# Retention and two feed-forward layers on one core: the layers in blocks of 384 tokens instead of 512 and 256

## The chip, the cores and the metric

The kernel runs on one core of a Trainium2 chip. The metric is the device time of one execution in microseconds (us). Engines are TensorE (PE in the rows; PEld is its weight load), VectorE (DVE), ScalarE (ACT), GpSimd (POOL) and SyncE (SP, which here only issues DMAs).

## The reference

A retention layer is followed by two feed-forward layers on 2304 tokens of 512 features.

```python
scores = scale * np.matmul(q, k.transpose(0, 1, 3, 2))      # 4 batches, 8 heads, 576 tokens, 64 wide
Dmat = np.where(rel >= 0, gamma[:, None, None] ** rel[None, :, :], 0.0)
x = np.matmul(scores * Dmat[None], v)                        # -> 2304 x 512
h = x @ w_in;  x = np.maximum(0.01 * h, h) @ w_out           # layer 1, d_ff 2048
h = x @ w_in2; out = (h - np.tanh(h)) @ w_out2               # layer 2, d_ff 2048
```

## The kernel before

**Arithmetic.** Each matmul operand is kept as a high and a low part (xh and xl; `w[:, 0]` and `w[:, 1]`; `g[:, 0]` and `g[:, 1]`), and each product is made of three matmuls: high by high, high by low, low by high.

**Tiling of the layers.** d_ff is 16 slices of 128, in 4 groups of 4 slices (`NG`, `GF`). A group `(m, g)` of layer `m` goes through all 2304 tokens in blocks; a step is one block and one slice `f`, so a block has 4 steps. Before the change a group has the token blocks 512, 512, 256, 512, 512 (five, 20 steps); the last group of all has the 256 at its end. The first group begins with six blocks of 256 (`EARLY`, `QW`), done two slices at a time during the retention (`unit_h`, `unit_o`), and goes on with one block of 256 and one of 512.

**A step.** `h_mm` (L194) makes h, 128 slice features by n tokens: 4 input chunks by 3 products, 12 matmuls n columns wide. `act_a` and `chain` make g from it. In layer 1 that is two ScalarE operations (L207, L208) and GpSimd's low part (L240). In layer 2, `act_a` has ScalarE's square, tanh and two more (L216 to L222) and GpSimd's product v (L218); `chain` has VectorE's subtraction (L233), product (L234) and predicated copy (L237), ScalarE's high part (L239) and GpSimd's low part (L240). `o_mm` (L266) adds the slice's share of the output in PSUM: in layer 1, 4 output chunks by 3 products, n columns wide; in layer 2, n/128 token chunks by 3 products, always 512 columns wide. After the fourth slice `evac` adds the sums into `acc` in SBUF (VectorE, L292; in a first group, copies at L288 and L290), in layer 1 n wide, in layer 2 always 512 wide. In layer 1's last group it also splits the result into xh (L296) and xl (L302); in layer 2's last it sends `acc` out.

**Order.** It is written out by hand (`manual_schedule`); each engine works through its queue in program order. In iteration s come `h_mm(s)`, `chain(s-1)`, `act_a(s)`, `o_mm(s-2)` (`LAG` is 2), up to four weight operations, `evac(s-2)`, the other weight operations, and the splits of weights. In the last four steps `act_a(s)` stands ahead of `chain(s-1)`, and the last four `o_mm` follow the last `h_mm`.

**Weights.** They come as 64-bit words and are narrowed by VectorE (L127 to L148) during layer 1, those of layer 2 partly to a scratch in DRAM and back (L163, L168). These operations are spread over the steps of a group. At its end each of the next group's 8 pieces is split: ScalarE's high part (L174), GpSimd's low part (L175), one piece in each of two steps, two in each of the next two, one in each of two more.

**Buffers.** PSUM has 3 tiles for h and 5 for the output sums, each 128 x 512; a g tile lives for three steps.

Of the kernel before, what the change touches and what calls it, by code (L numbers as in the profile page):

```python
# [33 lines left out]
def retention_moe_moe(  # L34
# [18 lines left out]
    NT, DM = out.shape  # L53
# [7 lines left out]
    NG = NF // GF  # L61
# [11 lines left out]

    QW, EARLY = 256, 6
    steps = []
    per_group = {}
    for m in range(2):
        for g in range(NG):  # L80
            big = [(t, 512) for t in range(0, NT - NT % 512, 512)]
            rest = [(NT - NT % 512, NT % 512)] if NT % 512 else []
            if (m, g) == (0, 0):
                blocks = [(t * QW, QW) for t in range(EARLY)]
                blocks += rest + [b for b in big if b[0] >= EARLY * QW]
            elif (m, g) == (1, NG - 1):
                blocks = big + rest
            else:
                blocks = big[:2] + rest + big[2:]
            first = len(steps)  # L90
            steps += [(m, g, t, n, f) for t, n in blocks for f in range(GF)]
            per_group[m, g] = (first, len(steps))
# [12 lines left out]
    def load_piece(key):  # L105
        m, kind, f = key
        src = ((w1i, w1o), (w2i, w2o))[m][kind][f]
        st = stage.tile([P, 512], I64 if wide else F32, tag="st", name="st")
        nc.sync.dma_start(out=st, in_=src)
        raw[key] = st  # L110
# [55 lines left out]
    def fetch_piece(key):  # L166
        w = cw_pool[0].tile([P, 512], F32, tag="cw", name="cw")
        nc.sync.dma_start(out=w, in_=kept.pop(key))  # L168
        half[key] = w

    def split_piece(key):
        wf = half.pop(key)
        wp = wring.tile([P, 2, 512], F32R, tag=f"w{key[1]}", name="wp")
        nc.scalar.activation(out=wp[:, 0, :], in_=wf, func=AF.Copy)  # L174
        nc.gpsimd.tensor_tensor(  # L175
            out=wp[:, 1, :], in0=wf, in1=wp[:, 0, :].bitcast(F32), op=ALU.subtract
        )
        wt[key] = wp

    def pieces_of(m, g):  # L180
        return [(m, kind, g * GF + f) for f in range(GF) for kind in range(2)]


    pools = {}
    hp, ga, tmp, ac_ps = {}, {}, {}, {}

    def h_mm(s):
        m, g, t0, n, f = steps[s]
        w = wt[m, 0, g * GF + f]
        ps = pools["h"](s)  # L190
        for kk in range(KK):
            cs = slice(kk * P, (kk + 1) * P)
            for i, (wi, x) in enumerate(((0, xh), (0, xl), (1, xh))):
                nc.tensor.matmul(  # L194
                    out=ps[:, :n], lhsT=w[:, wi, cs], rhs=x[:, kk, t0:t0 + n],
                    start=kk == 0 and i == 0, stop=kk == KK - 1 and i == 2,
                )
        hp[s] = ps

    def act_a(s):  # L200
        m, g, t0, n, f = steps[s]
        W, tp = pools["w"], pools["t"]
        h = hp[s][:, :n]
        if m == 0:
            a = tp.tile([P, W], F32, tag="u", name="a")
            gt = pools["g"].tile([P, 2, W], F32R, tag="g", name="g")
            nc.scalar.activation(out=a[:, :n], in_=h, func=AF.Prelu, alpha=0.01)  # L207
            nc.scalar.activation(out=gt[:, 0, :n], in_=h, func=AF.Prelu, alpha=0.01)  # L208
            tmp[s] = a, gt
            return  # L210
        u = tp.tile([P, W], F32, tag="u", name="u")
        v = tp.tile([P, W], F32, tag="v", name="v")
        t_ = tp.tile([P, W], F32, tag="t", name="t")
        q = tp.tile([P, W], F32, tag="q", name="q")
        mk = tp.tile([P, W], F32, tag="mk", name="mk")
        nc.scalar.activation(out=u[:, :n], in_=h, func=AF.Square)  # L216
        nc.scalar.activation(out=t_[:, :n], in_=h, func=AF.Tanh)  # L217
        nc.gpsimd.tensor_tensor(out=v[:, :n], in0=t_[:, :n], in1=u[:, :n], op=ALU.mult)  # L218
        nc.scalar.activation(  # L219
            out=q[:, :n], in_=u[:, :n], func=AF.Square, scale=math.sqrt(RHO_C), bias=qb[:, 0:1]  # L220
        )
        nc.scalar.activation(out=mk[:, :n], in_=u[:, :n], func=AF.Relu, bias=qb[:, 1:2])  # L222
        tmp[s] = (v, t_, q, mk)
# [83 lines left out]
    def split_order(keys):  # L307

        return sorted(keys, key=lambda k: (k[2] + LAG * k[1], k[1]))

    def piece_ops(keys, split=True, spare=()):


        ops, late = [], []
        for j, key in enumerate(keys):
            part = narrow_ops(key)
            if j + 2 < len(keys):
                part.append(lambda k=keys[j + 2]: load_piece(k))
            ops += part[:3] + late + part[3:]
            late = [lambda k=key: split_piece(k)] if split else []  # L320
            if key in spare:
                late = [lambda k=key: keep_piece(k)]
        return ops + late
# [303 lines left out]
    def layers():  # L627
        with ExitStack() as mc:
            pools["t"] = mc.enter_context(tc.tile_pool(name="t1", bufs=2))
            pools["g"] = mc.enter_context(tc.tile_pool(name="g1", bufs=3))  # L630
            cw_pool[0] = mc.enter_context(tc.tile_pool(name="c1", bufs=2 * GF + 3))
            ps_h = mc.enter_context(tc.tile_pool(name="ps_h1", bufs=3, space=PSUM))
            pools["h"] = lambda s: ps_h.tile([P, 512], F32, tag="h", name="h")
            pools["a"] = mc.enter_context(tc.tile_pool(name="ps_a1", bufs=5, space=PSUM))
            pools["w"] = 512
            early[0] = False

            plan, splits = {}, {}  # L640
            groups = list(per_group)
            free = n_early
            for q, nxt in zip(groups, groups[1:]):
                lo, hi = per_group[q]
                lo, last = max(lo, free), hi - GF
                keys = split_order(pieces_of(*nxt))

                kept_ones = [k for g in range(1, NG) for k in pieces_of(1, g)]
                a, b = (len(kept_ones) * (q[1] - i) // (NG - 2) for i in (1, 0))
                spare = kept_ones[max(a, 0):b] if q[0] == 0 and 0 < q[1] < NG - 1 else []  # L650
                if q[0]:
                    ops = [lambda k=k: fetch_piece(k) for k in keys]
                else:
                    ops = piece_ops(keys + spare, split=False, spare=spare)
                    plan.setdefault(lo, []).extend([lambda k=k: load_piece(k) for k in keys[:2]])
                free = max(hi if spare else last + 1, lo + 9)
                span = range(lo + 1, free)
                for j, op in enumerate(ops):
                    plan.setdefault(span[j * len(span) // len(ops)], []).append(op)
                for key in keys:  # L660
                    at = last + key[2] % GF + (1 if key[1] == 0 else 1 + LAG)
                    splits.setdefault(at, []).append(key)
            end = len(steps)
            for s in range(n_early, end):
                h_mm(s)
                tight = s >= end - GF
                if tight:
                    act_a(s)
                if s > n_early:
                    chain(s - 1)  # L670
                if not tight:
                    act_a(s)
                if n_early <= s - LAG < end - GF:
                    o_mm(s - LAG)
                ops = plan.get(s, [])
                for op in ops[:4]:
                    op()
                if n_early <= s - LAG < end - GF:
                    evac(s - LAG)
                for op in ops[4:]:  # L680
                    op()
                for key in splits.get(s, ()):
                    split_piece(key)

            for s in range(end - GF, end):
                o_mm(s)
                if s == end - GF:
                    chain(end - 1)
                evac(s)

    with tc.manual_schedule():
        retention()
        layers()
# [69 lines left out]
```

## Time and profile before

| what | us |
|---|---|
| median of 3 runs | 892.57 (891.94 to 893.65) |
| profiled execution | 891.21 |
| its span, first to last instruction | 889.4 |
| TensorE busy | 863.9 (97%) |
| VectorE, ScalarE, GpSimd busy | 532.8, 374.3, 422.5 |

Times in the timeline count from the start of the span. A matmul's own duration in the rows (389 ns at 512 columns) is its latency; matmuls overlap, so what one costs is read from start to start. The layers begin at about 162 us, layer 2 at about 488 us. "Idle before" in a row names the engine's waiting time and, behind the arrow, what ended it.

### The profile page before, as it was taken

Reading aid. Unit: us, or ns where it says so; the run is one execution under the profiler, and the core shown is the slowest. Engines: PE = TensorE matmul, PEld = TensorE weight load, DVE = VectorE, ACT = ScalarE, POOL = GpSimd, SP = SyncE. Lnnn points to the kernel's source line nnn. Section 1 sums busy time; section 2 is a strip of 40 time slices with the busy share of each in tenths; the row PEclk is TensorE's granted clock in tenths of the full one; section 3 lists DMA queues with packets and bytes.
Section 4 is the critical chain, followed back from the end, with each engine's and each line's share of the span. In section 5 each row is a group of like instructions: output and inputs, shape, how many; then the busy total and the mean of one; then the engine's idle time right before and its main releaser. Section 6 shows DMA issues by size and latency. Waiting matters only on the chain.

```text
span 889.4 us, 13456 instructions
## 1 busy us (share of the span) xinstructions
PE 863.9 (97%) x5152; PEld 740.8 (83%) x5152; DVE 532.8 (60%) x880; ACT 374.3 (42%) x751; POOL 422.5 (48%) x340
## 2 busy tenths in 40 slices
PE   6669999999999999999999999999999999999998
PEld 5669999988888889888888888888888888888886
DVE  6964343698888788865652555444545655555454
ACT  2333222242122212233324665675466555565553
POOL 4644432264233622363224644585457744585443
PEclk9989999999999999999999999999999999999999
DMA  8743342233464335531121200020001000001111
GB/s 299 237 141 118 108 132 78 71 108 106 131 185 149 120 128 148 173 107 48 48 83 39 57 1 1 8 76 13 1 1 47 13 1 1 1 1 48 48 48 71
DMA packets 28576, 70.97 MB, mean 80 GB/s; under 512 B 3297, under 2 KB 3681, under 8 KB 28513
## 3 DMA queue, kind: packets, MB, share of 16 engines
q1 hardware_dynamic: 27936, 69.74, 24.5%
q8 instruction: 40, 0.66, 0.3%
q10 hardware_dynamic: 576, 0.38, 0.1%
q14 instruction: 24, 0.19, 0.1%
HBM read 59.10 MB, written 11.01 MB: 79 GB/s over the span
## 4 chain that ended last, share of the span: by engine, by line
PE 92%; DVE 3%; ACT 1%; DMA 1%; POOL 1%; issue 1%; SPq 0%; ACTq 0%; POOLq 0%
PE h L194 41%; PE a L266 40%; PE a L541 4%; PE x_b L516 3%; PE o L463 1%; PE sc L402 1%; PE o L475 1%; DVE cw L148 1%; DVE pt L417 1%; DMA kv<-in_vn 1%; POOL wp L175 1%; PE x_c L435 1%; DMA qk<-in_qT 1%; PE x_a L408 0%; DVE st L445 0%
## 5 line engine op out<-in xcount | busy, mean ns | idle before, releaser
L194 PE MATMUL h<-xh,wp 128*128 128x512 f32 (+1 forms) x1184 | 355.2, 366 | 0.0
L194 PEld LDWEIGHTS h<-xh,wp 128*128 128x128 f32 x1184 | 216.1, 189 | 37.0
L194 PE MATMUL h<-xl,wp 128*128 128x512 f32 (+1 forms) x592 | 216.9, 366 | 0.0
L266 PE MATMUL a<-wp,g 128*128 128x512 f32 x864 | 209.4, 390 | 0.2 <-POOL g L240 0.2
L266 PEld LDWEIGHTS a<-wp,g 128*128 128x128 f32 x864 | 161.1, 188 | 33.8 <-POOL g L240 1.0
L266 PE MATMUL a<-g,wp 128*128 128x512 f32 (+1 forms) x816 | 175.6, 364 | 0.0
L240 POOL TENSOR_TENSOR g<-v,g 128x512 fp32r<-128x512 f32 (+1 forms) x80 | 94.8, 1186 | 144.6 <-ACT g L239 144.5
L266 PEld LDWEIGHTS a<-g,wp 128*128 128x128 f32 x816 | 141.4, 189 | 24.6
L240 POOL TENSOR_TENSOR g<-a,g 128x512 fp32r<-128x512 f32 (+1 forms) x68 | 88.0, 1294 | 154.9 <-ACT g L208 141.5
L207 ACT ACTIVATE a<-h 128x512 f32<-128x512 f32 (+1 forms) x68 | 37.3, 548 | 227.0 <-PE h L194 226.1
L175 POOL TENSOR_TENSOR wp<-cw,wp 128x512 fp32r<-128x512 f32 x64 | 90.9, 1430 | 76.1 <-ACT wp L174 75.7
L194 PEld LDWEIGHTS h<-xl,wp 128*128 128x128 f32 x592 | 111.6, 189 | 18.5
L148 DVE SCALAR_TENSOR_TENSOR cw<-st,cw 128x512 uint32<-128x512 uint32 x128 | 115.2, 900 | 3.8
L233 DVE TENSOR_TENSOR h<-h,t 128x512 f32<-128x512 f32 (+1 forms) x80 | 51.5, 644 | 107.3 <-ACT t L217 107.3
L292 DVE TENSOR_TENSOR acc<-a,acc 128x512 f32<-128x512 f32 (+1 forms) x114 | 73.8, 662 | 66.8 <-PE a L266 66.7
L239 ACT ACTIVATE g<-v 128x512 fp32r<-128x512 f32 (+1 forms) x80 | 47.1, 589 | 145.4 <-DVE v L237 144.3
L218 POOL TENSOR_TENSOR v<-t,u 128x512 f32<-128x512 f32 (+1 forms) x80 | 94.8, 1185 | 14.2 <-ACT t L217 13.8
L234 DVE SCALAR_TENSOR_TENSOR v<-q,v 128x512 f32<-128x512 f32 (+1 forms) x80 | 55.5, 694 | 55.2 <-POOL v L218 54.1
L237 DVE COPY_PREDICATED v<-mk,h 128x512 f32<-128x512 uint32 (+1 forms) x80 | 54.9, 686 | 8.2
L219 ACT ACTIVATE q<-u,qb 128x512 f32<-128x512 f32 (+1 forms) x80 | 54.5, 681 | 0.0
L222 ACT ACTIVATE mk<-u,qb 128x512 f32<-128x512 f32 (+1 forms) x80 | 54.2, 677 | 0.0
L216 ACT ACTIVATE u<-h 128x512 f32<-128x512 f32 (+1 forms) x80 | 43.6, 545 | 19.4 <-PE h L194 18.9
(60 smaller groups left out, 774.5 us busy)
## 6 DMA issues: line engine op xcount, KB each, us to landing
st<-in_w1i SPq DMA_DIRECT2D x16, 512.0 KB, 3.6
st<-in_w1o SPq DMA_DIRECT2D x16, 512.0 KB, 3.5
st<-in_w2i SPq DMA_DIRECT2D x16, 512.0 KB, 4.0
st<-in_w2o SPq DMA_DIRECT2D x16, 512.0 KB, 4.0
kept<-cw SPq DMA_DIRECT2D x24, 256.0 KB, 4.3
cw<-kept SPq DMA_DIRECT2D x24, 256.0 KB, 2.7
kv<-in_vn SPq DMA_DIRECT2D x16, 320.0 KB, 5.1
qk<-in_qT SPq DMA_DIRECT2D x16, 288.0 KB, 4.0
```

The lines of the kernel that those rows point to most:

```text
L148: nc.vector.scalar_tensor_tensor(out=t["w"], in0=t[src], scalar=scalar, in1=t["w"], op0=op, op1=ALU.bitwise_or)
L175: nc.gpsimd.tensor_tensor(out=wp[:, 1, :], in0=wf, in1=wp[:, 0, :].bitcast(F32), op=ALU.subtract)
L194: nc.tensor.matmul(out=ps[:, :n], lhsT=w[:, wi, cs], rhs=x[:, kk, t0:t0 + n], start=kk == 0 and i == 0, stop=kk == KK - 1 and i == 2,)
L218: nc.gpsimd.tensor_tensor(out=v[:, :n], in0=t_[:, :n], in1=u[:, :n], op=ALU.mult)
L219: nc.scalar.activation(out=q[:, :n], in_=u[:, :n], func=AF.Square, scale=math.sqrt(RHO_C), bias=qb[:, 0:1])
L222: nc.scalar.activation(out=mk[:, :n], in_=u[:, :n], func=AF.Relu, bias=qb[:, 1:2])
L233: nc.vector.tensor_tensor(out=h, in0=h, in1=t_, op=ALU.subtract)
L234: nc.vector.scalar_tensor_tensor(out=v, in0=q, scalar=RHO_A, in1=v, op0=ALU.add, op1=ALU.mult)
L237: nc.vector.copy_predicated(out=v, mask=mk.bitcast(U32), data=h)
L240: nc.gpsimd.tensor_tensor(out=gt[:, 1, :n], in0=v, in1=gt[:, 0, :n].bitcast(F32), op=ALU.subtract)
L266: nc.tensor.matmul(out=o, lhsT=l, rhs=r, start=f == 0 and i == 0 and d % pack == 0, stop=f == GF - 1 and i == 2 and (d + 1) % pack == 0, s ...
L292: nc.vector.tensor_tensor(out=dst, in0=a, in1=dst, op=ALU.add)
```

## The change

All groups of both layers have six blocks of 384 tokens, so 24 steps. The first group keeps its six early blocks of 256 and goes on with two of 384. The tiles of `act_a` and `chain` are 384 wide (`pools["w"]`). The last group has no block order of its own any more. All else in the code is the same; where the plan counts steps (weight operations, splits) it follows the new list.

```diff
--- before.py
+++ after.py
@@ -73,20 +73,15 @@
 
 
 
-    QW, EARLY = 256, 6
+    QW, EARLY, BW = 256, 6, 384
     steps = []
     per_group = {}
     for m in range(2):
         for g in range(NG):
-            big = [(t, 512) for t in range(0, NT - NT % 512, 512)]
-            rest = [(NT - NT % 512, NT % 512)] if NT % 512 else []
+            blocks = [(t, BW) for t in range(0, NT, BW)]
             if (m, g) == (0, 0):
-                blocks = [(t * QW, QW) for t in range(EARLY)]
-                blocks += rest + [b for b in big if b[0] >= EARLY * QW]
-            elif (m, g) == (1, NG - 1):
-                blocks = big + rest
-            else:
-                blocks = big[:2] + rest + big[2:]
+                narrow = [(t * QW, QW) for t in range(EARLY)]
+                blocks = narrow + [b for b in blocks if b[0] >= EARLY * QW]
             first = len(steps)
             steps += [(m, g, t, n, f) for t, n in blocks for f in range(GF)]
             per_group[m, g] = (first, len(steps))
@@ -632,7 +627,7 @@
             ps_h = mc.enter_context(tc.tile_pool(name="ps_h1", bufs=3, space=PSUM))
             pools["h"] = lambda s: ps_h.tile([P, 512], F32, tag="h", name="h")
             pools["a"] = mc.enter_context(tc.tile_pool(name="ps_a1", bufs=5, space=PSUM))
-            pools["w"] = 512
+            pools["w"] = BW
             early[0] = False
```

## Rows read from the trace of the kernel before

**Rows 1.** Page: granted clock by slice, and the last chain's shares by engine.
```profile
PEclk9989999999999999999999999999999999999999
...
PE 92%; DVE 3%; ACT 1%; DMA 1%; POOL 1%; issue 1%; SPq 0%; ACTq 0%; POOLq 0%
```

**Rows 2.** Timeline, TensorE, layer 1 (start us, us, engine, line, operation, xcount).
```profile
225.16 2.88 PE L266 MATMUL a<-g,wp 128*128 128x512 f32 x12
...
230.60 2.88 PE L266 MATMUL a<-g,wp 128*128 128x512 f32 x12
...
243.11 1.60 PE L266 MATMUL a<-g,wp 128*128 128x256 f32 x12
...
245.99 1.60 PE L266 MATMUL a<-g,wp 128*128 128x256 f32 x12
```

**Rows 3.** Last chain in order of time, at the groups' 256-wide blocks.
```profile
333.57 2.75 PE a L266 x12
...
432.23 2.75 PE a L266 x12
...
629.48 2.75 PE a L266 x12
...
727.80 2.75 PE a L266 x12
```

**Rows 4.** Timeline, layer 2, a block of 256: h and o matmuls, one turn.
```profile
540.75 0.28 PE L194 MATMUL h<-xh,wp 128*128 128x256 f32 x1
...
542.18 1.55 PE L266 MATMUL a<-wp,g 128*128 128x512 f32 x6
...
542.87 0.74 POOL L240 TENSOR_TENSOR g<-v,g 128x256 fp32r<-128x256 f32 x1 [1.55 <-ACT g L239]
...
543.57 0.74 POOL L218 TENSOR_TENSOR v<-t,u 128x256 f32<-128x256 f32 x1
...
544.34 0.42 DVE L234 SCALAR_TENSOR_TENSOR v<-q,v 128x256 f32<-128x256 f32 x1 [0.54 <-POOL v L218]
...
545.84 0.73 POOL L240 TENSOR_TENSOR g<-v,g 128x256 fp32r<-128x256 f32 x1 [1.54 <-ACT g L239]
```

**Rows 5.** Timeline, TensorE, retention: the 128-wide score matmuls and their successor.
```profile
93.22 1.16 PE L402 MATMUL sc<-qk 64*128 64x128 f32 x16
94.31 0.49 PE L408 MATMUL x_a<-bd,qk 128*128 128x128 f32 x2
```

**Rows 6.** Timeline, layer 2: one turn at 512, and an eviction.
```profile
664.26 1.30 POOL L240 TENSOR_TENSOR g<-v,g 128x512 fp32r<-128x512 f32 x1 [2.31 <-ACT g L239]
...
665.51 1.29 POOL L218 TENSOR_TENSOR v<-t,u 128x512 f32<-128x512 f32 x1
...
666.84 0.69 DVE L234 SCALAR_TENSOR_TENSOR v<-q,v 128x512 f32<-128x512 f32 x1 [0.95 <-POOL v L218]
...
669.09 2.88 PE L266 MATMUL a<-wp,g 128*128 128x512 f32 x12
669.13 1.29 POOL L240 TENSOR_TENSOR g<-v,g 128x512 fp32r<-128x512 f32 x1 [2.32 <-ACT g L239]
...
669.97 2.73 DVE L292 TENSOR_TENSOR acc<-a,acc 128x512 f32<-128x512 f32 x4 [1.58 <-PE a L266]
```

**Rows 7.** Timeline, layer 2: the two steps with two weight pieces each.
```profile
680.54 1.29 POOL L240 TENSOR_TENSOR g<-v,g 128x512 fp32r<-128x512 f32 x1 [0.45 <-ACT g L239]
...
686.17 1.29 POOL L240 TENSOR_TENSOR g<-v,g 128x512 fp32r<-128x512 f32 x1
...
688.75 1.76 DVE L234 SCALAR_TENSOR_TENSOR v<-q,v 128x512 f32<-128x512 f32 x1 [1.27 <-POOL v L218]
...
692.12 1.31 POOL L240 TENSOR_TENSOR g<-v,g 128x512 fp32r<-128x512 f32 x1 [0.46 <-ACT g L239]
```

**Rows 8.** Timeline, TensorE, where layer 2 begins.
```profile
504.82 3.15 PE L266 MATMUL a<-wp,g 128*128 128x512 f32 x12
```

**Rows 9.** Timeline, TensorE, end of the kernel.
```profile
882.61 2.83 PE L266 MATMUL a<-wp,g 128*128 128x512 f32 x11 [0.18 <-POOL g L240]
```

## Prediction

> **What bounds the kernel now.** I began with the chain that ended last and the granted clock [rows 1]: the chain is TensorE's for 92% of the span, and the clock is at its higher level, 2.4 GHz, in all slices but one near the start. Next the spacing of matmuls in the timeline [rows 2]. A step of 24 matmuls takes 230.60 - 225.16 = 5.44 us at 512 columns, 226.7 ns each, and 245.99 - 243.11 = 2.88 us at 256 columns, 120.0 ns each. The columns alone are 512/2.4 = 213.3 and 256/2.4 = 106.7 ns. What is left over is 13.3 ns in both: each matmul costs its columns and 13.3 ns, whatever its width. The same place in successive groups of layer 1 recurs after 98.66 us, of layer 2 after 98.32 us [rows 3]. Columns (2304 a group for each of 96 h and o matmuls in layer 1, at 2.4 GHz) and fixed parts alone give, for layer 1, 92.16 + 480 x 0.0133 = 98.56 us; for layer 2, h 46.08 + 240 x 0.0133 = 49.28 and o 216 x 0.2267 = 48.96, together 98.24 us. So TensorE has next to no gap in the layers that better cutting could win back.
>
> **The sum, part 1: matmuls.** The number of columns doesn't change (2304 tokens a group either way); the number of instructions does. A full group has 6 blocks instead of 5, so 4 steps more. Each added step brings 12 h matmuls and, in layer 1, 12 o matmuls. In layer 2 the o matmuls are 128 tokens by 512 whatever the block, 18 x 4 x 3 = 216 a group, before and after. The first group of layer 1 has two blocks behind the early ones before (256 + 512) and after (384 + 384), the same 8 steps. So 3 groups x 4 x 24 + 4 groups x 4 x 12 = 288 + 192 = 480 matmuls more, each at 13.3 ns: **+6.4 us**, all of it on the path, as TensorE waits for nothing there. This needs the fixed part at 384 columns, which the trace doesn't have. I take 13.3, as the widths on both sides show it. Bounds: the shortest 256-wide stretch is that of twelve h matmuls in layer 2, 542.18 - 540.75 = 1.43 us, 12.5 ns above their columns [rows 4]; the 128-wide score matmuls, 16 in 94.31 - 93.22 = 1.09 us [rows 5], take 68.1 ns, 14.8 above their columns. With 44 x 48 + 20 x 48 = 3072 matmuls of 384 after and 37 x 48 + 17 x 48 = 2592 of the other two before (34.6 us of fixed parts; blocks behind the early ones, h in both layers and o in layer 1), these give 38.4 - 34.6 = +3.8 and 45.5 - 34.6 = +10.9 us.
>
> The Trainium skill, "TensorE: Matmul & The Clock Gate", section "Back-to-back issue gap", puts the gap of warm matmuls at their columns and 2.5 ns; by it 480 more would be an estimated 1.2 us. The rows show 13.3 with a new weight load ahead of each matmul, so the measurement decides.
>
> **Part 2: the chain that feeds layer 2.** A shorter step leaves the other engines less time, so their cover has to be worked out. In layer 2 one loop runs through three engines: GpSimd's g(s) at L240, then v(s+1) at L218 behind it in its queue, VectorE at L234 and L237, ScalarE's copy at L239, and g(s+1). Between two evictions it turns freely and shows its own length: at 512 from 664.26 to 669.13, 4.87 us, in the parts g to v 1.25, v to VectorE 1.33, VectorE to g 2.29 [rows 6]; at 256 from 542.87 to 545.84, 2.97 us, in parts 0.70, 0.77, 1.50 [rows 4]. At 384 I take the middle of each: 0.98 + 1.05 + 1.89 = 3.92 us. TensorE's step is 12 x 0.1733 + 9 x 0.2267 = 2.08 + 2.04 = 4.12 us. So the loop fits, by 0.20 us a step instead of 5.44 - 4.87 = 0.57. (At 256 it did not fit: 2.97 against 1.44 + 1.36 = 2.80, but only for four steps.)
>
> Once a block VectorE has evictions ahead of the next subtraction. At 512 they start 0.88 us behind the o matmuls (669.09 to 669.97) and last 2.73 us for four [rows 6]. At 384 there are three; the last can start when the ninth matmul is done, 2.04 + 0.20, and ends about 2.90. Then the subtraction (about 0.5, an estimate from L234's 0.69 and 0.42 at the two widths [rows 4, 6]), then 1.89 to g, which lasts about 1.0 (1.29 and 0.73 there): g is there 6.3 us after those o matmuls began. Its own o matmuls come two steps later, at 8.24. **Spare: 1.9 us**, with 0.2 more on each of the next three steps until the following eviction. So a plain block doesn't stall.
>
> **Part 3: the weight switch in layer 2.** At each group's end GpSimd also has the next weights' low halves (L175), one a step in two steps, two a step in two, one in two more. They don't get narrower with the block. At 512 the two double steps take 686.17 - 680.54 = 5.63 and 692.12 - 686.17 = 5.95 us from g to g [rows 7], 0.19 and 0.51 over TensorE's step; the spare of the steps before covers that (the groups' recurrence leaves 0.1 us [rows 3]). In the second VectorE's L234 takes 1.76 instead of 0.69 us, because GpSimd began a piece just ahead of it: 1.07 us of waiting. In the first, both pieces follow VectorE's: 1.25 + 1.33 + 0.69 + 2 x 1.29 = 5.85, 0.22 above what was measured (the pieces, 512 wide like that g, overlap a little). At 384 the same is 0.98 + 1.05 + 0.56 + 2.58 - 0.22 = 4.95; the second is 3.92 + 1.07 = 4.99. They lose 0.83 and 0.87 against 4.12. Going in, the spare is 1.9, plus 0.2, less some 0.6 in the eviction step (an estimate: the single piece that falls there starts at about 2.9 on my scale, runs to 4.2, and holds VectorE's L234, due at 3.4, until 4.0): 1.45 us. 1.45 - 1.70 = -0.25: a stall of 0.25 us at each of the three switches inside layer 2, **+0.8 us**. Bounds: none, if the interpolations are 0.15 us a step too long; or 0.87 us more for every further step in which GpSimd gets ahead of VectorE.
>
> **Part 4: edges.** Where layer 2 begins, the last eviction of layer 1 also splits x, and TensorE waits already: the o matmuls at 504.82 last 3.15 us where 2.88 is usual, a stall of 0.27 [rows 8]. At 384 VectorE's burst shrinks by about a quarter, but so does the time to the next o matmuls, from 10.88 to 8.28 us; an estimate in the same proportions puts the low half some 0.6 us late: **+0.3 us**. At the end the last block becomes 384 wide instead of 256. Now the o matmuls of its last two steps wait: the last eleven on record begin at 882.61 behind a wait for g [rows 9]. At 226.7 ns each all 24 would have taken 5.44 us from the last h matmul's end at about 879.3; they take 882.61 + 11 x 0.2267 - 879.3 = 5.8 to 6.0: about 0.5 us lost. At 384 each of these steps has nine o matmuls for cover instead of six (2.04 against 1.36 us), and the chain grows by less: **-0.5 us**. Evictions of layer 1 have 5 PSUM tiles for 4 in use, as at 512; from the first eviction's end to the first reuse of its tile there are 5.44 + 0.68 - 1.57 = 4.5 us at 512 and 4.16 + 0.52 - 1.28 = 3.4 at 384, and VectorE's narrowing of weights (L127 to L148) is spread over 24 steps instead of 20 in nearly the same time. I cost this at nothing, up to +1 us if VectorE comes late once. SP's loads, the scratch copies and the wait lists change in no other way.
>
> **Sum:** 6.4 + 0.8 + 0.3 - 0.5 = +7.0 us. The profiled run took 891.21 us (1.8 us around its span of 889.4, which the change leaves alone), so 898.2 for such a run; the median of the runs shown is 892.57, 1.4 higher, and from it the forecast is **899.6 us**.
>
> **Rivals.** (a) The weight switch costs more: GpSimd gets ahead of VectorE in one or two further steps of each switch. I have VectorE first by only about 0.2 us there; below that, it loses 1.07 us, 0.87 net. Three switches: +2.6 or +5.2, so 902.2 to 904.8. For it speaks that row of 1.76 us; against it, that a late ScalarE keeps the pieces late too. (b) The loop is longer than 4.12 us at 384 and becomes the bound of layer 2. If VectorE's and ScalarE's part kept its 512 length, 2.29, the loop would be 4.32, 0.20 over; 96 steps lose 19 us, less the spare of 1.9, in place of part 3's 0.8: 916. Decides from 0.20 us a step. Against it: every part shrinks in proportion between 512 and 256. (c) Not slower: the fixed part isn't the same at 384. The equal 13.3 could have two causes, at 256 the pace at which weight loads follow one another, at 512 something else, and a middle width could pay neither in full. It decides at (34.6 - 0.6)/3072 = 11.1 ns, where gain and stalls meet at 892.6; at 10 ns the time is 892.57 - 3.9 + 0.6 = 889.3. Against it: 14.8 at 128 columns, and no row of full weight loads below 12.5. The change does what it says: the counts follow from the lists of blocks. (d) Not slower either: the added matmuls cost only a few ns each, because most of their fixed part falls into time that the narrower ones leave elsewhere. The time is 892.57 + 480 x c + 0.6; it can't be told from no change up to c = 2.5 ns, where it is 894.4. Against it: TensorE's groups leave 0.1 us of such time in 98.6 [rows 3]. The page quoted in part 1 would have c at 2.5.
>
> **How the numbers follow.** Forecast (898.3 to 901.0, with the stalls of part 3 between none and triple): 0.66. (a) 0.18. (b) 0.07. (c) 0.07, of it 0.03 faster and 0.04 within 0.2% (1.8 us, about what a measurement of this kernel can tell from no change). (d) 0.02. So faster 0.03, same 0.06, slower 0.91. The range 897.0 to 905 takes in the forecast, (a) and the bounds of the fixed part (892.57 + 3.8 + 0.6 and + 10.9 + 0.6), and leaves out (b), (c) and (d), 0.16.
>
> **What would show it.** After: 384-wide steps of layer 1 every 4.16 us, of layer 2 every 4.12; groups recurring after 99.9 and 98.9 us and a little; TensorE's waits for g at L240 up from 0.2 us, standing at the first steps of layer 2's groups; no wait for g at the end. I'm wrong if matmuls of 384 aren't 173 ns apart, or if waits for g stand in every block.

## The result, and the profile after

The changed kernel takes 905.65 us (median of 5 runs, 903.80 to 907.19), the kernel before 893.20 beside it: ratio 1.0139, 95% interval 1.0118 to 1.0160. A later group of runs gave 904.22 against 892.70, ratio 1.0130 (1.0115 to 1.0145). So the change costs 11.5 to 12.5 us. The forecast was 899.6, with a range to 905: the sign is right, the size is not, and none of the four rivals had the reason. The second median lies inside the range, but by luck (see the end of the account below).

The page of after, its rows of the granted clock and of the last chain:

```profile
PEclk9789999999999999999999999999999999999999
...
PE 91%; DVE 4%; ACT 2%; POOL 1%; issue 1%; DMA 0%; POOLq 0%; ACTq 0%
```

As before [rows 1], TensorE holds the end, at 2.4 GHz but for the retention. The starts of its matmuls divide the span in two:

| stretch, us | before | after | difference | forecast |
|---|---|---|---|---|
| retention, to the layers' first h matmul | 161.90 | 163.88 | +1.98 | 0 |
| from there to the last matmul's start | 723.14 | 735.26 | +12.12 | +7.0 |
| rest of the span | 4.35 | 4.37 | +0.02 | 0 |

The second stretch hardly varies: in the repeated run of the same kernel it is 735.29. It is what the experiments below are compared by; "layers" means this stretch of the profiled run.

In it, the distance from each matmul's start to the next can be set against its columns at 2.4 GHz and 13.3 ns (13.33 in the sums). What is over goes into three heaps: distances more than 60 ns over (waits), the first twelve matmuls behind a change of width, and the rest.

| layers, us | before | after | difference |
|---|---|---|---|
| columns and 13.3 ns each | 721.69 | 728.09 | +6.40 |
| waits | 0.69 | 0.90 | +0.21 |
| first twelve behind a change of width | 0.69 | 6.15 | +5.46 |
| rest | 0.07 | 0.12 | +0.05 |

The first line is a count: it holds the forecast's own 13.3 ns for 480 more matmuls, so it must give the forecast's first term. What is measured is the last line: where widths are equal in a row, next to nothing is left beyond it, at 384 columns too. The third line was not in the forecast. In the timeline it is seen like this: layer 1 of after, where h and o are both 384 wide (start us, us, engine, line, operation, count):

```profile
170.15 2.24 PE L261 MATMUL a<-g,wp 128*128 128x384 f32 x12
...
174.31 2.24 PE L261 MATMUL a<-g,wp 128*128 128x384 f32 x12
```

and layer 2, where h is 384 and o is 512 wide:

```profile
562.00 2.24 PE L261 MATMUL a<-wp,g 128*128 128x512 f32 x9
564.09 0.33 PE L189 MATMUL h<-xh,wp 128*128 128x384 f32 x1
...
566.19 2.24 PE L261 MATMUL a<-wp,g 128*128 128x512 f32 x9
```

Layer 1's step is 174.31 - 170.15 = 4.16 us, as forecast. Layer 2's is 566.19 - 562.00 = 4.19 instead of 4.12: nine o matmuls take 2.09 instead of 2.04, twelve h matmuls 2.10 instead of 2.08. The distances from start to start, in ns, show where in the run this lies:

```
o, 512 wide, behind h of 384 (227 in a row of equal width):  230 233 236 224 231 236 228 232 231
h, 384 wide, behind o of 512 (173 in a row of equal width):  171 175 178 185 175 182 173 174 173 173 174 173
```

Behind each change the matmuls are unsteady for some six to nine, 41 ns late in sum going to 512 and 26 ns going to 384. With both in each of layer 2's steps that is 0.067 us a step. Before, only the 256-wide blocks changed width: 27 ns going from 256 to 512 and 7 ns gained on the way back.

### The profile page after: what moved, and what is told of

Read it like the earlier page. It is cut to its first block, busy times and chain, and to the rows that moved or that the text cites. A ratio compares the mean times of both kernels' runs of the same rounds, so it can differ in the third digit from the quotient of the medians.

```text
span 903.5 us, 14739 instructions
## 1 busy us (share of the span) xinstructions
PE 880.3 (97%) x5632; PEld 832.6 (92%) x5632; DVE 544.6 (60%) x947; ACT 385.8 (43%) x856; POOL 425.6 (47%) x384
## 4 chain that ended last, share of the span: by engine, by line
PE 91%; DVE 4%; ACT 2%; POOL 1%; issue 1%; DMA 0%; POOLq 0%; ACTq 0%
PE h L189 40%; PE a L261 39%; PE a L536 3%; PE x_b L511 3%; PE o L470 1%; PE o L458 1%; PE sc L397 1%; DVE cw L143 1%; DVE pt L412 1%; PE x_c L430 1%; POOL wp L170 1%; DVE acc L287 0%; DVE st L440 0%; DVE xl L480 0%; PE x_c L470 0%
## 5 line engine op out<-in xcount | busy, mean ns | idle before, releaser
L189 PE MATMUL h<-xh,wp 128*128 128x384 f32 x1408 | 387.1, 336 | 0.0
L189 PE MATMUL h<-xl,wp 128*128 128x384 f32 x704 | 235.8, 335 | 0.0
L261 PE MATMUL a<-g,wp 128*128 128x384 f32 x960 | 179.3, 334 | 0.0
L235 POOL TENSOR_TENSOR g<-a,g 128x384 fp32r<-128x384 f32 x80 | 88.9, 1111 | 175.8 <-ACT g L203 135.8
L235 POOL TENSOR_TENSOR g<-v,g 128x384 fp32r<-128x384 f32 x96 | 97.9, 1019 | 156.2 <-ACT g L234 154.2
L287 DVE TENSOR_TENSOR acc<-a,acc 128x384 f32<-128x384 f32 (+1 forms) x126 | 73.4, 611 | 69.6 <-PE a L261 69.6
L213 POOL TENSOR_TENSOR v<-t,u 128x384 f32<-128x384 f32 x96 | 97.6, 1017 | 6.7 <-ACT t L212 6.2
L229 DVE SCALAR_TENSOR_TENSOR v<-q,v 128x384 f32<-128x384 f32 x96 | 60.4, 629 | 60.4 <-POOL v L213 60.4
L214 ACT ACTIVATE q<-u,qb 128x384 f32<-128x384 f32 x96 | 59.2, 616 | 0.0
L217 ACT ACTIVATE mk<-u,qb 128x384 f32<-128x384 f32 x96 | 58.8, 613 | 0.0
```

The lines of the kernel that those rows point to most:

```text
L189: nc.tensor.matmul(out=ps[:, :n], lhsT=w[:, wi, cs], rhs=x[:, kk, t0:t0 + n], start=kk == 0 and i == 0, stop=kk == KK - 1 and i == 2,)
L214: nc.scalar.activation(out=q[:, :n], in_=u[:, :n], func=AF.Square, scale=math.sqrt(RHO_C), bias=qb[:, 0:1])
L229: nc.vector.scalar_tensor_tensor(out=v, in0=q, scalar=RHO_A, in1=v, op0=ALU.add, op1=ALU.mult)
L235: nc.gpsimd.tensor_tensor(out=gt[:, 1, :n], in0=v, in1=gt[:, 0, :n].bitcast(F32), op=ALU.subtract)
L261: nc.tensor.matmul(out=o, lhsT=l, rhs=r, start=f == 0 and i == 0 and d % pack == 0, stop=f == GF - 1 and i == 2 and (d + 1) % pack == 0, s ...
L287: nc.vector.tensor_tensor(out=dst, in0=a, in1=dst, op=ALU.add)
```

## The experiments

**The changed kernel again.**

> The changed kernel again, beside the others of this group. Question: is the retention's part of its loss (first h matmul of the layers at 163.88 us in its profile, 161.90 before) a property of the change? Theory 'chance of the clock': the code of the retention is the same, its TensorE clock falls to 1.2 GHz once in some executions and three times in others; so the runs split in two groups about 2 to 3 us apart by granted clock (0.996 and 0.991), and the kernel before does so too. Rival 'caused by the change': all of its runs have the lower clock, none of before's. In a run with the clock at 0.996 I expect 903.8 us, in one at 0.991 906 to 907.

Measured: 903.96 to 904.30 us; first h matmul at 162.50, layers 735.29. The kernel before, beside it, ran from 890.97 to 894.04, at mean clocks from 0.988 to 0.996. I had expected two groups of times, told apart by the mean clock, and in these runs there are none (893.27 us at 0.988, 893.61 at 0.995); but the retention's length moves on its own, in both kernels. Which stretches of it ran slower stands in the windows (stretch, us; busy us of PE, PEld, DVE, ACT, POOL with their counts; granted clock; DMA share; GB/s). Before, only 55 to 66 us is below 1.00, at 0.69. After, three stretches are:

```profile
22.00:33.00 11.00, 9.42 (x114) 8.56 (x112) 8.92 (x22) 5.01 (x14) 5.73 (x6) 0.69 0.76 276
33.00:44.00 11.00, 9.12 (x110) 8.69 (x108) 9.97 (x23) 2.72 (x8) 5.30 (x5) 0.84 0.58 197
...
55.00:66.00 11.00, 7.31 (x66) 6.61 (x68) 4.39 (x10) 2.81 (x7) 2.51 (x2) 0.69 0.25 77
```

The control with the blocks of before (e4, below) has the same three, and its first h matmul comes at 164.73:

```profile
22.00:33.00 11.00, 8.73 (x92) 7.91 (x94) 9.19 (x23) 4.50 (x13) 4.87 (x5) 0.69 0.60 215
33.00:44.00 11.00, 8.78 (x102) 8.14 (x100) 9.94 (x20) 3.23 (x8) 7.02 (x5) 0.84 0.65 225
...
55.00:66.00 11.00, 6.49 (x48) 5.85 (x50) 5.11 (x12) 2.81 (x6) 2.52 (x2) 0.69 0.17 53
```

Over all eleven profiled runs the first h matmul comes at 161.73 to 164.73 us, earliest in one with layer 2 in blocks of 384 and latest in this control. So the 1.98 us of the retention in the profiled pair are not the change's. How much of them the clock makes stays open: e3 (below) comes 1.1 us later than this repeated run, at nearly the same granted clocks in its slow stretches (0.85 and 0.69 against 0.84 and 0.69). The table of the layers stands without it.

**Layer 1 alone, layer 2 alone.** The list of blocks is chosen by layer:

```diff
-            blocks = [(t, BW) for t in range(0, NT, BW)]
+            if m == 0:      # e2_layer2: m == 1
+                blocks = [(t, BW) for t in range(0, NT, BW)]
...
+            else:
+                blocks = big[:2] + rest + big[2:]
```

> Only layer 1 has blocks of 384, layer 2 has 512 and 256 as before. Theory 'fixed part and changes of width': 3 groups x 96 = 288 matmuls more at 13.3 ns, +3.8 us, less some 0.1 us a group for the changes of width that the 256 blocks brought: +3.5 us against before; 384-wide steps every 4.16 us. Rival 'the loss is in layer 1' (its evictions or its weight narrowing come late): +8 us or more.

> Only layer 2 has blocks of 384, layer 1 has 512 and 256 as before. Theory 'changes of width': 192 matmuls more at 13.3 ns are +2.6 us; besides, each step goes from h matmuls of 384 to o matmuls of 512 and back, and the matmuls behind each change come late by 26 and 41 ns in sum, 0.067 us a step, 96 steps: +6.4; with a stall or two of 0.1 to 0.5: +9 us against before. Rival 'fixed part alone' (the rest of the loss is the retention's clock): +2.6 to +3 us.

Measured: layer 1 alone 895.27 us, 1.0034 of before (1.0022 to 1.0046); layers 726.61, that is +3.47 against +3.5 expected. Layer 2 alone 902.14, ratio 1.0112 (1.0093 to 1.0131); layers 732.79, +9.65 against +9. Of these, 2.56 are the added matmuls, 6.02 are lateness (6.71 instead of 0.69; 6.34 of it behind the 190 changes between 384 and 512, 41 and 26 ns each as above), and 1.10 are waits (1.79 instead of 0.69, most of them where layer 2 begins). The loss beyond the fixed parts is layer 2's, and "fixed part alone" falls.

**Half as many changes.** TensorE's order in layer 2 goes in pairs of steps, in the changed kernel and, as a control, in the one before:

```diff
-                if n_early <= s - LAG < end - GF:
-                    o_mm(s - LAG)
+                due = [s - LAG]
+                if steps[s][0] == 1:
+                    due = [s - LAG - 1, s - LAG] if (s - per_group[1, 0][0]) % 2 else []
+                due = [r for r in due if n_early <= r < end - GF]
+                for r in due:
+                    o_mm(r)
```

> The changed kernel with TensorE's order in layer 2 in pairs of steps: two steps' h matmuls, then two steps' o matmuls. The matmuls are the same, the changes of width half as many. Theory 'changes of width': 48 x 0.067 = 3.2 us faster than the changed kernel; two steps every 8.31 us instead of 8.37. Rival 'in layer 2 matmuls of these widths are slower as such' (by their operands' places or by traffic of the other engines): no change, within 0.5 us. Rival 'the chain of g bounds layer 2': no change in the steps either, though TensorE's waits would fall.

> Control for the pairs: the kernel before with the same order of TensorE in layer 2 (two steps' h, two steps' o). There h and o are both 512 wide except in one block of five. Theory 'changes of width': nothing to gain but half of some 27 ns a step in 16 steps, so -0.2 us, the same as before within 0.5 us. Rival 'the order in pairs helps by itself' (weights stay longer, more time for g): -3 us here too.

Measured: the pairs take 902.55 us beside the changed kernel's 904.22; layers 732.71, 2.55 less, where 3.2 were expected. (As medians the two are only 1.67 apart; the first h matmul comes at 163.63 here and at 162.50 in the repeated run.) The timeline has two steps in 8.31 us, as expected:

```profile
563.85 4.28 PE L261 MATMUL a<-wp,g 128*128 128x512 f32 x18
...
572.16 4.28 PE L261 MATMUL a<-wp,g 128*128 128x512 f32 x18
```

Lateness behind changes falls from 6.15 to 3.13 us, 42 and 25 ns for each of half the changes; 0.47 us come back as longer waits where layer 2 begins. The control takes 892.81, ratio 0.9998 (0.9989 to 1.0007), layers 723.31, +0.17: the order in pairs gains nothing where h and o are equally wide.

**A quarter, and twice as many.** In fours, with 4 and 4 PSUM tiles, five g tiles and two weight splits moved a step or two later (these lines of the edit are left out below); and in halves, six h, three o, six h, six o:

```diff
-                    due = [s - LAG - 1, s - LAG] if (s - per_group[1, 0][0]) % 2 else []
+                    due = range(s - LAG - 3, s - LAG + 1) if (s - per_group[1, 0][0]) % 4 == 3 else []
```

```diff
-                h_mm(s)
+                    h_mm(s, 0)
+                    o_mm(s - LAG, 0)
+                    h_mm(s, 1)
...
-                    o_mm(s - LAG)
+                    o_mm(s - LAG, 1 if halves else None)
```

> The changed kernel with TensorE's order in layer 2 in fours: four steps' h matmuls, then four steps' o matmuls (PSUM 4 and 4 tiles instead of 3 and 5, five g tiles instead of three, two weight splits a step or two later). A quarter of the changes of width. Measured from the first h matmul of the layers to the last matmul, where the changed kernel takes 735.26 us and the pairs 732.71. Theory 'changes of width': 23 x 0.067 = 1.5 us of late matmuls instead of 6.15, so 4.6 us less, 730.7, if no new stall comes (up to +1 us where layer 2 begins, as in the pairs). Rival 'the pairs gained by giving g more time': nothing more to gain, 732.7.

> The changed kernel with layer 2's steps interleaved more finely: 6 h matmuls, 3 o, 6 h, 6 o. Twice the changes of width, the same matmuls. From the starts in the changed kernel's trace the first 3 and 6 matmuls of 512 behind a change come 19 and 30 ns late in sum, the first 6 of 384 26 ns: 19 + 30 + 52 = 101 ns a step instead of 67. Theory 'changes of width, each with the lateness that its first matmuls show': +3.2 us, 738.5 us from the first h matmul to the last matmul. Rival 'a fixed price per change': +6.3 us, 741.6. Rival 'layer 2's matmuls are slow as such': 735.3.

Measured: the fours take 936.96 us, layers 766.90, far from the 730.7 expected. Lateness behind changes is 1.52 us, as expected (39 and 25 ns for each of 47 changes); but by the starts TensorE now waits 36 us. The profile counts an engine's idle time only from the end of a matmul's latency; of that it puts 22.5 us down to evictions (who waited for whom: us in total, times, longest):

```profile
PE a L261 <- DVE acc L287: 15.9, 16, 1.9
PE a L261 <- DVE acc L285: 6.6, 7, 1.9
```

The last o matmuls of a block and the first of the next stand back to back there, and with three sums in four tiles the next block waits for the evictions. That was an oversight of mine; as a time the run says nothing on the theory, as a count of late matmuls it agrees.

The halves take 908.80 us, layers 739.06, close to the 738.5 of the theory, but not by its way. Waits grow from 0.90 to 4.20 us; the likely reason, not tested, is that three of each step's o matmuls now come six h matmuls, about a microsecond, sooner. The lateness is 6.68 us for 369 changes: 23.5 ns each going to 512, as expected (24.5), but 12.6 going to 384 where I had taken 26. The two kinds of change to 384 differ: behind three o matmuls the next six h matmuls are 21 ns late in sum, behind six o matmuls only 4 ns, while behind 9, 18 and 36 it is 25 to 26. So there is no fixed price per change, and the lateness seen behind one length of run can't be carried over to another. The nearness of the total is chance.

**Equal widths in layer 2.** Each block of 384 computes 512 columns of h; the 128 added ones are read by nobody.

```diff
+        lo, wd = (min(t0, NT - 512), 512) if m == 1 else (t0, n)
...
-                    out=ps[:, :n], lhsT=w[:, wi, cs], rhs=x[:, kk, t0:t0 + n],
+                    out=ps[:, :wd], lhsT=w[:, wi, cs], rhs=x[:, kk, lo:lo + wd],
```

> The changed kernel, but layer 2's h matmuls are 512 columns wide: each block of 384 computes 128 columns more that nobody reads. Blocks, operands, order and o matmuls stay as they are; only the widths of h and o are now equal. From the first h matmul of the layers to the last matmul the changed kernel takes 735.26 us, of it 6.15 us late matmuls behind changes of width. The added columns cost 96 x 12 x 128/2.4 ns = 61.4 us. Theory 'changes of width': the lateness goes, 735.26 + 61.4 - 6.15 = 790.5, less some 0.5 as the waits for g get cover: 790 to 790.6, with steps of 12 x 226.7 + 9 x 226.7 ns = 4.76 us. Rival 'it is the alternation of operands' (g as weights, then as w, in blocks of 384): the lateness stays, 796.2 to 796.7 us and steps of 4.82 us.

Measured: 959.68 us; layers 789.77 us, where 790 to 790.6 were expected and 796.2 or more by the rival. Columns and fixed parts make 789.53 of it, with no wait, and lateness only in the few places where the widths of layer 1 and layer 2 meet. The step is 4.76 us, each matmul 226 or 227 ns behind the one before from the first on:

```profile
600.18 2.20 PE L262 MATMUL a<-wp,g 128*128 128x512 f32 x9
604.94 2.20 PE L262 MATMUL a<-wp,g 128*128 128x512 f32 x9
```

Same blocks, operands and order; the widths are equal, and the lateness is gone. The step is longer as well, and no matmul of layer 2 is 384 wide any more; but layer 1's matmuls of 384 in a row aren't late, in this run either (the rest is 0.06 us in all). So it is the change from one width to the other that makes it. With the longer step no wait for g is left either.

**The fixed part by itself.** The kernel before with groups 1 to 3 of layer 1 in blocks of 256:

```diff
+            elif m == 0:
+                blocks = [(t, QW) for t in range(0, NT, QW)]
```

> The kernel before with groups 1 to 3 of layer 1 in nine blocks of 256: 4 blocks x 4 steps x 24 x 3 groups = 1152 matmuls more, no change of width inside these groups. Theory 'a fixed part of 13.3 ns per matmul, whatever the width': +15.4 us, less 0.3 for the changes of width that go: +15.1. Rival 'a limit of weight loads at short matmuls': steps longer than 2.88 us, +18 or more; rival 'the fixed part is partly the step's': +12 or less.

Measured: 907.71 us, ratio 1.0163 (1.0149 to 1.0177), layers 738.47: +15.33 against +15.1. 1152 matmuls at 13.3 ns are 15.4; the steps are 2.88 us, and both rivals fall:

```profile
302.02 1.60 PE L268 MATMUL a<-g,wp 128*128 128x256 f32 x12
304.90 1.60 PE L268 MATMUL a<-g,wp 128*128 128x256 f32 x12
```

## Why the prediction was wrong, point by point

**Part 1, the matmuls: right.** 480 more matmuls make +6.40 us, as the fixed part at 384 is the 13.3 taken from 512 and 256 (layer 1's step of 4.16 us is 24 x 173.3 ns). With that rivals (c) and (d) fall. The ends of its range (12.5 and 14.8) weren't needed, and the lower one was misread: see next.

**The step that failed** is "each matmul costs its columns and 13.3 ns, whatever its width", carried from stretches of one width [rows 2] into part 2's step of layer 2, 12 x 0.1733 + 9 x 0.2267 = 4.12 us, where the widths alternate. It is 4.19, and over 96 steps, less what before had of it, 5.46 us are missing from the sum. The rows had it: the six o matmuls at 542.18 [rows 4] span 1.55 us with the last one's 0.39, so they are (1.55 - 0.39)/5 = 232 ns apart and not 227. I used that row only for the twelve h matmuls ahead of it, whose 12.5 ns were the other face of the same thing (256 behind 512 starts early), and took them for a lower bound of the fixed part. Before the change 16 of layer 2's 80 steps alternated widths; after it, all 96. A stretch that exists before, but in few steps, has to be read as closely as the one that fills the time.

**Part 2, the chain of g: right.** GpSimd's g and the eviction step in layer 2 of after:

```profile
642.69 1.02 POOL L235 TENSOR_TENSOR g<-v,g 128x384 fp32r<-128x384 f32 x1 [1.93 <-ACT g L234]
...
646.62 1.01 POOL L235 TENSOR_TENSOR g<-v,g 128x384 fp32r<-128x384 f32 x1 [1.93 <-ACT g L234]
...
650.03 2.24 PE L261 MATMUL a<-wp,g 128*128 128x512 f32 x9
...
655.26 1.02 POOL L235 TENSOR_TENSOR g<-v,g 128x384 fp32r<-128x384 f32 x1 [2.74 <-ACT g L234]
```

One turn takes 646.62 - 642.69 = 3.93 us (forecast 3.92), g starts 655.26 - 650.03 = 5.23 us behind the o matmuls of the eviction (the forecast had g there after 6.3, which is a start after 5.3 and its own length of 1.0), and the spare is 8.37 - 6.25 = 2.1 instead of 1.9, because two steps are 0.13 longer. Rival (b) falls.

**Part 3, the weight switch: mechanism and terms right, the stall smaller.** The double steps of the first switch:

```profile
593.11 1.02 POOL L235 TENSOR_TENSOR g<-v,g 128x384 fp32r<-128x384 f32 x1 [0.18 <-ACT g L234]
...
598.05 1.02 POOL L235 TENSOR_TENSOR g<-v,g 128x384 fp32r<-128x384 f32 x1
...
600.08 1.63 DVE L229 SCALAR_TENSOR_TENSOR v<-q,v 128x384 f32<-128x384 f32 x1 [1.76 <-POOL v L213]
...
603.04 1.02 POOL L235 TENSOR_TENSOR g<-v,g 128x384 fp32r<-128x384 f32 x1 [0.17 <-ACT g L234]
```

4.94 and 4.99 us, where 4.95 and 4.99 were forecast, and VectorE's product waits in the second (1.63 us) as in [rows 7]. TensorE stalls 0.11 us at one switch of the three, instead of 0.25 at each. The forecast's own terms, 1.9 + 0.2 - 0.6, add up to 1.5 and not to its 1.45, which takes 0.05 off each; and TensorE's longer step gives back some 0.07 us a step (an estimate from 4.19 against 4.12), so a sum that stood on the edge came out near nothing. In the eviction step ahead of the double steps the product takes 1.57, 1.09 and 1.09 us at the three switches, 1.0, 0.5 and 0.5 above its 0.56, where the forecast had held it for 0.6. Rival (a) falls: in no further step of the switches does GpSimd get ahead of VectorE.

**Part 4: where layer 2 begins, about right; the end, wrong.** The o matmuls at 507.19 last 2.64 us where 2.24 is usual, a stall of 0.4 instead of before's 0.27 [rows 8]; forecast 0.6. At the end, 36 o matmuls stand in one row with a wait of 0.37 us in all by their starts, against 0.45 in the kernel before; I had expected the wait to go.

```profile
507.19 2.64 PE L261 MATMUL a<-wp,g 128*128 128x512 f32 x9
...
890.75 8.78 PE L261 MATMUL a<-wp,g 128*128 128x512 f32 x36
...
893.49 1.02 POOL L235 TENSOR_TENSOR g<-v,g 128x384 fp32r<-128x384 f32 x1
893.57 1.35 DVE L229 SCALAR_TENSOR_TENSOR v<-q,v 128x384 f32<-128x384 f32 x1 [0.83 <-POOL v L213]
...
896.33 1.01 POOL L235 TENSOR_TENSOR g<-v,g 128x384 fp32r<-128x384 f32 x1 [1.83 <-ACT g L234]
```

The last step's product (893.57) comes 0.08 us behind GpSimd's g of the step before, and takes 1.35 us instead of the 0.56 that it takes in most steps; the last g comes that much later. I had let the chain grow with its width and left out who runs beside it. The Trainium skill says in "SBUF — State Buffer", section "Who interferes with whom", that a VectorE instruction with two SBUF inputs contends with a GpSimd instruction that reads SBUF, and that the order of issue decides which of the two waits. The trace agrees, here with 0.8 us of VectorE's. In the kernel before VectorE came first at this place, by 0.04 us, and it was GpSimd's g that took longer, 0.97 us instead of 0.73:

```profile
881.54 0.42 DVE L234 SCALAR_TENSOR_TENSOR v<-q,v 128x256 f32<-128x256 f32 x1 [0.56 <-POOL v L218]
881.58 0.97 POOL L240 TENSOR_TENSOR g<-v,g 128x256 fp32r<-128x256 f32 x1
```

**The retention** was rightly left out: its 1.98 us in the profiled pair go with stretches of lower granted clock, and as late a start of the layers, with the same stretches, occurs with the blocks of before too.

In sum, of the 12.12 us of the layers 7.0 were forecast: 6.40 came as matmuls (6.4), 0.21 as waits (0.6 in parts 3 and 4), and 5.46 as lateness behind changes of width (0). 12.1 us on the 892.57 us that the forecast started from make 904.7, which is still inside the range; but what put it there would have been luck, as the range reached so far for rival (a) and a larger fixed part.

## What to carry to other kernels

Read a matmul's price from a stretch whose neighbours are like those it will have: equal widths in a row ran at columns and 13.3 ns here, while steps that alternated 384 and 512 cost 0.067 us more each. Blocks that divide the tokens evenly aren't for that reason cheaper: with 13.3 ns for each matmul the fewest and widest win, even with a remainder block. Where widths must alternate, longer runs of each width help (pairs took back 3.0 of 6.15 us of lateness, with 0.5 returned as waits), as long as the output tiles are enough for blocks that stand back to back.

## What was not expected of the hardware

Behind a change of the matmuls' width TensorE's starts are uneven for six to nine matmuls, also with weight loads on record as far ahead as usual (each begins as the previous matmul starts) and without a wait: 41 ns late in sum from 384 to 512, 27 from 256 to 512, 26 from 512 to 384, and 7 early from 512 to 256. The sums depend on how long the runs are: 18 ns for three matmuls of 512, and for six of 384 21 ns behind three of 512 but 4 behind six. That the change of width causes it is shown by the equal-width run; why, and what sets the pattern, stays open.
